# Attention plus gated FFN on one core: score banks from full-array matmuls on masked queries, spare matmuls placed by weighted streaming, other order constants, and ten split row blocks for three

## The chip, the cores and the metric

The kernel runs on one core of one Trainium2 chip. The metric is the device time of one execution in microseconds; the median of three runs before the change is 1193.59 us (1193.0 to 1194.12). The engines are TensorE (PE, with its weight loads shown apart as PEld), VectorE (DVE), ScalarE (ACT), GpSimd (POOL) and SyncE (SP), which issues the DMAs.

## The reference

```python
def _A_ref(x, wqkv, wo):                      # B=1, S=2048, D=512, H=32, Dh=16
    qkv = transpose((x @ wqkv).reshape(B, S, 3, H, Dh), 2, 0, 3, 1, 4)
    q, k, v = qkv[0], qkv[1], qkv[2]
    scores = einsum("bhqd,bhkd->bhqk", q, k) * (Dh ** -0.5)
    p = softmax(scores, axis=-1)
    o = einsum("bhqk,bhkd->bhqd", p, v)
    return transpose(o, 0, 2, 1, 3).reshape(B, S, D) @ wo

def _B_ref(x, w1, w3, w2):                    # F=1792
    h = silu(x @ w1) * (x @ w3)
    return h @ w2

xn = layernorm(x)                             # over the last axis, eps 1e-5
out = x + _A_ref(xn, wqkv, wo) + _B_ref(xn, w1, w3, w2)
```

All tensors are bfloat16. There are 32 heads of width 16, so the scores are 32 x 2048 x 2048 numbers: 2048 blocks of 128 x 512 per pass. The kernel computes them twice: once with the queries on the partitions, to find each row's maximum, and once with the keys on the partitions, for the exponentials.

## The kernel before

**Layout.** Heads go in 8 groups of four. KT and QT hold a group's four heads in four bands of 32 partitions: 16 for the head's width, then two rows (ones in KT, minus the row maximum as a high and a low part in QT), the rest without effect. A matmul on one band uses a quarter of the array's rows (a "row" matmul, 32 x 128), and up to four such can run side by side. Everything else (projections, FFN, output, and the product of probabilities and values) uses the whole array's rows (a "col" matmul); the last of these has four column bands of 17.

**Units.** The queries are cut into 4 chunks of 512 by 8 head groups; each is cut into units of 256 queries, or of 128 in the first group and the last four. This makes 73 units; units 0, 1 and 57 to 72 have 128 queries. A block of a unit is named (128-row block of queries, head).

**The two passes of a unit.** First pass (`p1_cand`, L1013): two row matmuls (L1059) write two PSUM banks of 512 scores each, and VectorE reduces both with one maximum (L1099) into `part`. Banks 0 to 3 serve this pass, two at a time. GpSimd then joins the four partial maxima (L1195 to L1215, six small operations), writes them as two rows into Z, a DMA transposes Z, and two DMAs put the rows into QT (keys QTr0 and QTr1; the marker `("AUG", u)`). The first two and the last four units take a quicker way over VectorE and TensorE (`tile_QT2`, L804). Second pass (`p2_cand`, L1281): row matmuls (L1321) write scores minus maximum, keys on the partitions, into one of banks 4 to 7; ScalarE takes the exponential into one of 34 slots of PT (L1334), or of two neighbouring banks at once when both are ready (`exp_pair`, L1364). `score_bank` (L1268) chooses the bank; MATE is how much earlier a bank next to the last queued one is treated as free (TAIL_MATE, 0.3 us, does the same after the last reduce). `tile_PV` (L1373) multiplies with the values (L572); ScalarE moves the result to U (L1428), and GpSimd normalises it with reciprocals that travel over DRAM (L1453, L1473).

**Split blocks.** For the block (1, 3) of some units (SPLIT, L344) the maximum over 2048 keys is found otherwise: two banks get the differences of two key quarters (`d_cand`, L1127: L1155 and L1158 with the negated queries QN from GpSimd), ScalarE applies Relu into RB (L1168), and a fused VectorE operation adds RB to two quarters of the scores and takes the maximum (L1088). The other head of the pair is reduced alone, two banks at a time (kind "Q"). Four reduces become two plus one fused operation.

**Tiles.** K and Q projections, V, the FFN pairs (G and U), outputs and PV are `_Tile`s of col matmuls, one of banks 4 to 7 each. `choose` (L1522) picks the next; the FFN pairs are spread over the first pass by FFN_LO and FFN_HI, and their results wait in 24 tiles of hT (NHT) for the output matmuls.

**Order.** One program writes every engine's instruction list before the launch. The loop at L1877 asks each engine's picker for its next candidate with an estimated start, and appends the earliest. Every engine runs its list strictly in order with semaphore waits. On TensorE (`pick_pe`, L1717) the candidates are: a first-pass pair a, a second-pass bank b, a split difference d, a tile's next col matmul c, and a spare matmul f (`fill_cand`, L1688: `ident` times `xnT` into a free bank; nothing reads it). Spare matmuls keep up TensorE's activity: `note_load` counts the columns that were streamed, `low_load` says whether a spare one is wanted, and `recent_cols` under RECENT_MIN lets c (which may be the spare one) go first though a row matmul is due. A_LEAD and ROW_LEAD are how early the row matmuls are due before VectorE and ScalarE need them; PACE spreads the output tiles. On GpSimd `pick_pool` (L1849) takes the first item of the queues z, ln, nx, split, nrm, ffn and pad that can start soonest.

Of the kernel before, what the change touches and what calls it, by code (L numbers as in the profile page):

```python
# [8 lines left out]
ALU = mybir.AluOpType  # L9
# [4 lines left out]
_COLD = 5.9  # L14
_VIS = {"dve": 0.138, "pool": 0.085}
# [21 lines left out]
class _Prog:  # L37
# [3 lines left out]
    def __init__(self):  # L41
        self.ops = {e: [] for e in _ENGS}
        self.reg = {}
        self.ndma = 0
        self.dma_last = [None] * _NDMA_SEMS
        self.dma_final = [0] * _NDMA_SEMS
        self.free = {e: 0.85 for e in _ENGS}
        self.rg = [0.0] * 4
        self.pe_mode = "col"
        self.pe_full = True  # L50
        self.pe_vis = 0.0
        self.act_end = 0.0
# [83 lines left out]
    def pe(self, fn, reads, writes, mode, groups, dur, name="", first=None):  # L136
# [117 lines left out]
def _build(nc, A_x, A_wqkv, A_wo, B_w1, B_w3, B_w2, out):  # L254
# [21 lines left out]
    LAZY_GAP = 0.02  # L276
# [37 lines left out]
    FFN_HI = 800  # L314
# [7 lines left out]
    LOAD_RATE = 5000.0  # L322
    LOAD_CAP = 3000.0
    LOAD_MIN = 3000.0
    RECENT = 2.9
    RECENT_MIN = 9800.0
# [3 lines left out]
    SPLIT_LO = 40  # L330
    SPLIT_END = 12
    SPLIT_STEP = 6
# [21 lines left out]
    with ctx:  # L354
# [5 lines left out]
        stats = sb("stats", [128, NT, 6], FP32)  # L360
        mv = sb("mv", [128, NT, 2], FP32)
        lnr = sb("lnr", [128, NT], FP32)
        lnb = sb("lnb", [128, NT], FP32)
        lnt = sb("lnt", [128, NT], FP32)
# [30 lines left out]
        U = sb("U", [128, NUB, 256], FP32)  # L395
        R = sb("R", [128, 2, 256], FP32)
# [58 lines left out]
        poolq = {k: [] for k in ("z", "ln", "nx", "split", "nrm", "ffn", "pad")}  # L455
# [22 lines left out]
        P.op("dve", lambda e: e.memset(wq_last[:, :, :], 0.0), writes=[("wq7",)], occ=0.3 * NPADQ)  # L478
        P.op("dve", lambda e: e.memset(bank(7), 0.0), writes=[("ps", 7)], occ=0.5)
# [533 lines left out]
        def p1_cand():  # L1013
# [42 lines left out]
            def emit():  # L1056
                def f(e):
                    for i, (j, c_) in enumerate(cells):
# [4 lines left out]
                P.pe(f, reads, writes, "row", rows, _c_mm(512) * (3 - len(rows)), name="p1_%d" % n, first="dve")  # L1063
                p1_n[0] += 1
                tokens[0] = min(tokens[0] + PACE, PACE_CAP)
                note_load(st, 1024)
# [60 lines left out]
        def d_cand():  # L1127
# [22 lines left out]
            def emit():  # L1150
# [11 lines left out]
                note_load(st, 1024)  # L1162
# [7 lines left out]
            return st, emit, rd, n  # L1170

# [109 lines left out]
        def p2_cand():  # L1281
# [17 lines left out]
            kb, j = rest[best[1]]  # L1299
            k0 = kb * kpb  # L1300
            reads = (qh_keys(qs, q0, nq, (j,)) + qt_keys(qs, q0, nq, "QTr0") + qt_keys(qs, q0, nq, "QTr1")
# [3 lines left out]
            st = P.pe_start("row", (j,), rd)  # L1305
            sl = pt_free[0]

            def emit():
                rest.pop(best[1])
# [16 lines left out]
                P.pe(f, reads, writes, "row", (j,), _c_row(nq, kpb), name="p2_%d" % n, first="act")  # L1326
                note_load(st, 512)
# [194 lines left out]
        def choose():  # L1522
# [9 lines left out]
            if outs and ok(outs[0]) and exp_unit[min(pv_u[0], NU - 1)] <= 14:  # L1532
                return outs.pop(0)
            if ffn and ok(ffn[0]):
                return ffn.pop(0)
# [52 lines left out]
        def col_cand():  # L1588
# [20 lines left out]
            def emit_part(k):  # L1609
# [11 lines left out]
                note_load(st, t.cols // 4 * k)  # L1621

            def emit():
# [5 lines left out]
                note_load(st, t.cols if t.cols < 2048 else t.cols * left // 512)  # L1629
# [22 lines left out]
        level = [0.0, 0.0]  # L1652
        recent = []

        def load_at(st):
            return level[1] - LOAD_RATE * max(0.0, st - level[0])

        def note_load(st, w):
            level[1] = min(LOAD_CAP, max(load_at(st), -LOAD_CAP) + w)
            level[0] = max(st, level[0])  # L1660
            recent.append((st, w))

        def recent_cols(st):
            while recent and recent[0][0] < st - 4.0:
                recent.pop(0)
            return sum(w for t, w in recent if t >= st - RECENT)

        def low_load(st):
            return load_at(st) < LOAD_MIN

        def warm_cand():
            for bk in (5, 4):
# [5 lines left out]
                def emit():  # L1678
# [4 lines left out]
                    note_load(st, 1024)  # L1683
# [4 lines left out]
        def fill_cand():  # L1688
# [16 lines left out]
            def emit_part(k):  # L1705
# [3 lines left out]
                note_load(st, 512 * k)  # L1709
                n_fill[0] += 1  # L1710
            return st, lambda: emit_part(4), _c_mm(512), emit_part, 4
        n_fill = [0]

# [3 lines left out]
        def pick_pe():  # L1717
# [12 lines left out]
            end = max(P.free["pe"], max(P.rg))  # L1730
            rows = []
# [12 lines left out]
            def go(x):  # L1744
                def f():
                    couple[0] = x[0]
                    x[1]()
                return x[0], f
# [9 lines left out]
            if p1_n[0] >= NP1 and b is not None:  # L1758
# [118 lines left out]
        while True:  # L1877
            assign()
            split_prep()
            best = None  # L1880
# [10 lines left out]
        P.n_fill = n_fill[0]  # L1891
        P.n_pair = n_pair[0]
# [65 lines left out]
```

## Time and profile before

| what | value |
|---|---|
| median of 3 runs | 1193.59 us |
| the profiled execution's span | 1191.2 us |
| TensorE busy | 1122.5 us (94%), mean granted clock 0.998 |
| VectorE busy | 1173.5 us (99%) |
| ScalarE busy | 1167.5 us (98%) |
| GpSimd busy | 455.5 us (38%) |
| DMA | 52.07 MB, 44 GB/s in the mean |

The span goes from the first to the last instruction of one profiled execution; the runs' times include what lies around it, and are about 2.4 us longer here. Busy time counts every moment in which at least one instruction of an engine is in flight, so an engine whose instructions overlap at their ends can look full while it could still take more. In a row of groups stand line, engine, operation, output and inputs with their shapes, the count, busy time, mean duration in ns, and the idle time before it with what ended it. In a row of windows stand the stretch and its length, then the busy time and count of PE, PEld, DVE, ACT and POOL (of those that ran, when one line is asked for), the granted clock of TensorE, and the DMA's share and rate. In a row of waits stand who waited for whom, total us, times, and the longest.

### The profile page before, as it was taken

The numbers are of one execution on the slowest core, as the hardware profiler recorded it, in microseconds if no ns is written. First come the engines' busy times: TensorE is split into PE (matmuls) and PEld (weight loads), VectorE is DVE, ScalarE is ACT, GpSimd is POOL, SyncE is SP. The second block draws the span as 40 slices with busy tenths as digits, with TensorE's granted clock in tenths as the row PEclk, the third lists the DMA queues.
The fourth block names the chain that finished last, engine by engine and source line by source line (L and its number), as shares of the span: only waits on it lengthen the run. The fifth ranks groups of instructions, "written<-read, shape, count | busy, mean of one in ns | idle before, by whom it ended". The sixth has DMA issues, their size and how long they took to land.

```text
span 1191.2 us, 33351 instructions
## 1 busy us (share of the span) xinstructions
PE 1122.5 (94%) x13807; PEld 477.7 (40%) x13964; DVE 1173.5 (99%) x1079; ACT 1167.5 (98%) x2223; POOL 455.5 (38%) x910
## 2 busy tenths in 40 slices
PE   9999999999999999999999999999899999998997
PEld 4433333333334333333333334343333333345554
DVE  8999999999999999999999999999999999999995
ACT  7899999999999999999999999999999999999998
POOL 5363743433432255344422236634222124333320
PEclk9999999999999999999999999999999999999999
DMA  6523222111111021111100122211000111000000
GB/s 185 124 62 86 66 65 80 39 33 42 36 25 38 24 70 43 36 37 29 35 20 25 36 53 49 48 42 37 23 20 15 36 28 42 24 19 20 19 18 22
DMA packets 130779, 52.07 MB, mean 44 GB/s; under 512 B 99788, under 2 KB 130628, under 8 KB 130628
## 3 DMA queue, kind: packets, MB, share of 16 engines
q1 hardware_dynamic: 130628, 49.94, 16.9%
q8 instruction: 109, 1.79, 0.6%
q14 instruction: 42, 0.34, 0.1%
HBM read 38.67 MB, written 6.74 MB: 38 GB/s over the span
## 4 chain that ended last, share of the span: by engine, by line
ACT 43%; PE 28%; DVE 22%; issue 2%; DMA 2%; POOL 1%; SPq 0%; ACTq 0%; another core or an unknown queue 0%; POOLq 0%
ACT PT L1334 29%; DVE part L1099 22%; PE ps L568 11%; PE ps L1321 8%; ACT PT L1364 7%; PE ps L1059 5%; PE ps L572 4%; ACT zg L867 1%; ACT th L861 1%; ACT U L1428 1%; DMA R<-rd 1%; ACT ub L871 1%; ACT kq L756 1%; DMA rd<-Rc 1%; ACT xnT L677 1%
## 5 line engine op out<-in xcount | busy, mean ns | idle before, releaser
L1099 DVE TENSOR_REDUCE part<-ps 128x2 f32<-128x1024 f32 x1018 | 1153.2, 1257 | 1.5 <-PE ps L1059 1.3
L1334 ACT ACTIVATE PT<-ps 128x512 bf16<-128x512 f32 x1660 | 879.2, 627 | 4.7 <-PE ps L1321 1.7
L1321 PE MATMUL ps<-QT,KT 32*128 32x256 bf16 (+1 forms) x4672 | 544.5, 259 | 10.7 <-ACT PT L1364 4.7
L1059 PE MATMUL ps<-KT,QT 32*128 32x512 bf16 x2042 | 423.9, 383 | 4.4 <-DVE part L1099 3.1
L1321 PEld LDWEIGHTS ps<-QT,KT 32*128 32x128 bf16 x4672 | 206.9, 92 | 214.9 <-issue 110.3
L1453 POOL TENSOR_TENSOR Rc<-Lc,mone 128x8 f32<-128x8 f32 (+1 forms) x69 | 105.0, 1522 | 287.2 <-DMA Lc<-U 287.1
L1364 ACT ACTIVATE PT<-ps 128x1024 bf16<-128x1024 f32 x194 | 204.4, 1078 | 0.0
L568 PE MATMUL ps<-xnT,ident 128*128 128x512 bf16 (+3 forms) x576 | 159.1, 335 | 26.1 <-DVE part L1099 6.3
L572 PE MATMUL ps<-PT,Vaug 128*17 128x256 bf16 (+1 forms) x4672 | 177.3, 261 | 4.2 <-ACT PT L1334 1.6
L1059 PEld LDWEIGHTS ps<-KT,QT 32*128 32x128 bf16 x2042 | 107.3, 91 | 122.8 <-DVE part L1099 56.7
L568 PE MATMUL ps<-xnT,w 128*128 128x512 bf16 (+3 forms) x597 | 143.8, 316 | 9.8 <-ACT U L1428 4.4
L572 PEld LDWEIGHTS ps<-PT,Vaug 128*17 128x17 bf16 x4672 | 82.2, 89 | 89.5 <-issue 68.9
L568 PEld LDWEIGHTS ps<-xnT,ident 128*128 128x128 bf16 x642 | 47.0, 97 | 99.4 <-ACT PT L1334 44.2
L568 PEld LDWEIGHTS ps<-xnT,w 128*128 128x128 bf16 x637 | 44.9, 97 | 85.7 <-issue 53.0
L568 PE MATMUL ps<-w,hT 128*128 128x512 bf16 (+3 forms) x312 | 72.1, 311 | 3.3 <-ACT U L1428 2.1
L848 POOL TENSOR_TENSOR a<-zg,ub 128x512 f32<-128x512 bf16 x56 | 64.6, 1154 | 21.8 <-ACT ub L871 21.5
L850 POOL TENSOR_TENSOR hT<-a,t 128x512 bf16<-128x512 f32 x56 | 71.0, 1268 | 2.4
L1206 POOL TENSOR_TENSOR mx<-part 128x16 f32<-128x16 f32 (+1 forms) x67 | 14.2, 211 | 140.5 <-DVE part L1099 140.2
L1473 POOL TENSOR_TENSOR wk_on<-U,R 128x256 bf16<-128x256 f32 (+1 forms) x36 | 22.9, 637 | 81.3 <-DMA R<-rd 81.2
L846 POOL TENSOR_SCALAR t<-th 128x512 f32<-128x512 bf16 x56 | 34.8, 622 | 43.8 <-ACT th L861 42.2
L1473 POOL TENSOR_TENSOR on_b<-U,R 128x256 bf16<-128x256 f32 (+1 forms) x33 | 23.4, 710 | 72.5 <-DMA R<-rd 72.4
L861 ACT ACTIVATE th<-zg 128x512 bf16<-128x512 bf16 x56 | 37.6, 671 | 0.0
(105 smaller groups left out, 552.2 us busy)
## 6 DMA issues: line engine op xcount, KB each, us to landing
w<-in_B_w_dram SPq DMA_DIRECT2D x112, 128.0 KB
R<-rd SPq DMA_DIRECT2D x55, 128.0 KB
QT<-qd SPq DMA_DIRECT2D x31, 128.0 KB
KT<-kd SPq DMA_DIRECT2D x28, 128.0 KB
PT<-in_A_x_dram SPq DMA_DIRECT2D x4, 512.0 KB
xr<-in_A_x_dram SPq DMA_DIRECT2D x16, 128.0 KB
out_dram<-osb SPq DMA_DIRECT2D x16, 128.0 KB
qd<-kq SPq DMA_DIRECT2D x15, 128.0 KB
```

Source lines behind the costliest of these rows:

```text
L568: return e.matmul(bank(bk)[:, c0 + a:c0 + b], make_lhsT(0, 128), rhs_ap(0)[:, a:b], start=start, stop=stop, **kw)
L572: ins = e.matmul(bank(bk)[32 * i:32 * i + m, c0 + a:c0 + b], make_lhsT(i), rhs if (a, b) == (0, ncols) else rhs[:, a:b], start=start, stop ...
L848: q.append(_Item(lambda e: e.tensor_tensor(a32[:, :], zg[:, ss, :], ub[:, ss, :], ALU.mult), [("zg", ss), ("ub", ss)], [("a32",)], 1.1, 1.25))
L850: q.append(_Item(lambda e: e.tensor_tensor(hT[:, hslot(idx), :], a32[:, :], t1[:, :], ALU.mult), [("a32",), ("t1",)], [("hT", hslot(idx))] ...
L861: lazyq.append(_Item(lambda e: e.activation(th[:, ss, :], zg[:, ss, :], ACTF.Tanh), [("zg", ss)], [("th", ss)], 0.52, cb=part_done))
L1059: ins = e.matmul(bank(2 * sl + i), QT[32 * j:32 * j + 32, qs, q * 128:(q + 1) * 128], KT[32 * j:32 * j + 32, g, c_ * 512:(c_ + 1) * 512], ...
L1099: redq.append(_Item(lambda e: e.tensor_reduce(dst, pair_ap.rearrange("p (a b) -> p a b", b=512), AX.X, ALU.max), writes, [("part", par, qt ...
L1321: ins = e.matmul(bank(b)[:, i * nq:(i + 1) * nq], KT[32 * j:32 * j + 32, g, (k0 + i) * 128:(k0 + i + 1) * 128], QT[32 * j:32 * j + 32, qs, ...
L1334: expq.append(_Item(lambda e: e.activation(PT[:, sl, :], bank(b), ACTF.Exp, scale=SCALE), [("ps", b)], [("PT", sl)], _c_act(512), cb=cb, e ...
L1364: return _Item(lambda e: e.activation(PT[:, s0:s1 + 1:s1 - s0, :], ps8[:, b0:b1 + 1:b1 - b0, :], ACTF.Exp, scale=SCALE), [("ps", b0), ("ps ...
L1453: poolq["nrm"].append(_Item(lambda e: e.tensor_tensor(Rc[:, pp, 0:nl], Lc[:, pp, 0:nl], mone[:, 0:nl], ALU.pow), [("Lc", pp), ("mone",)], ...
L1473: poolq["nrm"].append(_Item(lambda e: e.tensor_tensor(onorm[ob][:, g, q0:q0 + nq], U[:, us, 0:nq], R[:, pp, 0:nq], ALU.mult), [("U", us)] ...
```

## The change

The scores of a second-pass bank may also be made by a col matmul over all 128 rows: KT of all four heads against BD, a copy of the unit's QT in which the bands of the other three heads are zero. GpSimd makes four copies for each unit but the last four (`bd_prep`), two units' worth at a time, with a mask `hmask` that is written at the start. Such a wide bank (`p2_cand(True)`) is taken in place of the row bank when the recent activity is under HEAT_WIDE, or after a col matmul when ScalarE soon needs a bank and the first pass is not due.

Activity is now a weighted mean of streaming over the last 2.0 us (`heat`): 0.794 for each row band, 2.36 for banded col matmuls, 2.16 for full ones. A spare matmul is wanted while it is below HEAT_FILL = 1.5. HEAT_FORCE = 0 takes the place of RECENT_MIN, HEAT_P1 = 0 leaves the repeated first-pass matmuls unused, and HEAT_TILE = 9.0 lets FFN tiles go.

The split units go from 20 on in steps of 4 (before: from 40 in steps of 6). Some order constants change, hT has 22 tiles instead of 24, and the statistics of the layer norm lie in U.

```diff
+_HEAT_ROW, _HEAT_COL, _HEAT_FULL = 0.794, 2.36, 2.16
...
+        w = _HEAT_ROW * len(groups) if mode == "row" else _HEAT_FULL if self.pe_full else _HEAT_COL
+        self.heat.append((start, start + dur, w))
...
-    LAZY_GAP = 0.02
+    LAZY_GAP = 0.1
...
-    MATE = 0.0
+    MATE = 0.2
...
-    A_LEAD = 0.69
-    RELAX = 0.03
-    PACE = 4500
-    PACE_CAP = 6000
-    NHT = 24
+    A_LEAD = 0.76
+    RELAX = 0.0
+    PACE = 7000
+    PACE_CAP = 9000
+    NHT = 22
...
-    FFN_HI = 800
+    FFN_HI = 880
...
-    LOAD_RATE = 5000.0
-    LOAD_CAP = 3000.0
-    LOAD_MIN = 3000.0
-    RECENT = 2.9
-    RECENT_MIN = 9800.0
+    RECENT = 2.0
+    HEAT_FILL = 1.5
+    HEAT_TILE = 9.0
+    HEAT_P1 = 0
+    AGAIN = 3
+    HEAT_FORCE = 0
+    HEAT_WIDE = 1.1
...
-    SPLIT_LO = 40
+    BD_ON = 1
+    BD_END = 4
+    BD_NEAR = 0.35
+    WIDE_LEAD = 0.45
+    W_WAIT = 0.02
+    OUT_GATE = 14
+    SPLIT_LO = 20
     SPLIT_END = 12
-    SPLIT_STEP = 6
+    SPLIT_STEP = 4
...
+        BD = sb("BD", [128, 2, 4, 256], BF16)
...
+        hmask = sb("hmask", [128, 4], FP32)
...
+        P.op("dve", lambda e: e.memset(hmask[:, :], 0.0), writes=[("hmask",)], occ=0.07)
+        def head_masks(e):
+            for j in range(4):
+                ins = e.memset(hmask[32 * j:32 * j + 32, j:j + 1], 1.0)
+            return ins
+        P.op("dve", head_masks, writes=[("hmask",)], occ=0.26)
...
+        def bd_prep():
+            u = bd_next[0]
+            if u >= NU - BD_END:
+                return
+            if ("AUG", u) not in done or (u >= 2 and p2_u[0] <= u - 2):
+                return
+            bd_next[0] += 1
+            qc, g, q0, nq = units[u]
+            qs = (qc * NG + g) % 3
+            if p2_u[0] > u:
+                return
+            for j in (2, 3, 0, 1):
+                poolq["bd"].append(_Item(
+                    lambda e, j=j: e.tensor_scalar(BD[:, u % 2, j, 0:nq], QT[:, qs, q0:q0 + nq], hmask[:, j:j + 1], 0.0,
+                                                   ALU.mult, ALU.add),
+                    [("hmask",)] + qh_keys(qs, q0, nq) + qt_keys(qs, q0, nq, "QTr0") + qt_keys(qs, q0, nq, "QTr1"),
+                    [("BD", u % 2, j)], 0.12 + nq / 1000.0, cb=lambda op, j=j: done.add(("BD", u, j))))
...
-        def p2_cand():
+        def p2_cand(wide=False):
...
+            whole = ()
+            if BD_ON and u < NU - BD_END:
+                whole = [k for k, (kb, j) in enumerate(rest[:4]) if ("BD", u, j) in done]
+            if wide and not whole:
+                return None
...
+            st = P.pe_start("col", None, rd) if wide else P.pe_start("row", (j,), rd)
...
+                if wide:
+                    parts = [col_groups(b, lambda i, z=32, a=a: KT[:, g, (k0 + a) * 128 + 32 * i:(k0 + a) * 128 + 32 * i + z],
+                                        lambda i: BD[:, u % 2, j, 0:nq], nq, c0=a * nq,
+                                        own=P.pe_mode == "col" and not P.pe_full) for a in range(kpb)]
...
+        def heat(st):
+            h = P.heat
+            while h and h[0][1] < st - 6.0:
+                h.pop(0)
+            return sum(w * (min(b_, st) - max(a_, st - RECENT)) for a_, b_, w in h
+                       if b_ > st - RECENT and a_ < st) / RECENT
         def low_load(st):
-            return load_at(st) < LOAD_MIN
+            return heat(st) < HEAT_FILL
...
+            if b is not None and red_n[0] < NP1 and heat(max(end, b[2])) < HEAT_WIDE:
+                w = p2_cand(True)
+                if w is not None:
+                    b = w
+                    warm = True
...
+            if b is not None and P.pe_mode == "col" and not warm:
+                w = p2_cand(True)
+                if w is not None:
+                    near = max(P.free["dve"] + sum(it.occ for it in redq) - A_LEAD, a[2]) if a is not None else 1e9
+                    if near > max(w[0], end) + BD_NEAR:
+                        if w[0] <= end + W_WAIT and P.free["act"] + 0.476 * len(expq) - WIDE_LEAD <= w[0]:
+                            return w[0], w[1]
+                        if x is b and not fits(c, late + TOL):
+                            return w[0], w[1]
             k = fits(c, late + TOL)
-            if not k and recent_cols(c[0]) < RECENT_MIN and c[0] <= end + URG_WAIT:
+            if not k and heat(c[0]) < HEAT_FORCE and c[0] <= end + URG_WAIT:
                 k = min(2, c[4]) if len(c) > 3 else 9
...
-            for k in ("z", "ln", "nx", "split", "nrm", "ffn", "pad"):
+            for k in ("z", "ln", "nx", "split", "bd", "nrm", "ffn", "pad"):
```

More of the change, by code (lines that the diff above doesn't have):

```diff
@@ L454, in _build @@
         dveq = []
[L455 removed]
+        poolq = {k: [] for k in ("z", "ln", "nx", "split", "bd", "nrm", "ffn", "pad")}
         spq = []
@@ L1056, in emit @@
             def emit():
+                again = 1
+                if n >= N_HEAD and kind == "R":
+                    slack = P.free["dve"] + sum(it.occ for it in redq) - st - 0.25
+                    while again < AGAIN and heat(st) + 0.35 * (again - 1) / RECENT < HEAT_P1 and slack > (again + 1) * _c_mm(512):
+                        again += 1
                 def f(e):
-                    for i, (j, c_) in enumerate(cells):
+                    for i, (j, c_) in list(enumerate(cells)) * again:
                         ins = e.matmul(bank(2 * sl + i), QT[32 * j:32 * j + 32, qs, q * 128:(q + 1) * 128],
@@ L1325, in f, with fw @@
                     return ins
-                P.pe(f, reads, writes, "row", (j,), _c_row(nq, kpb), name="p2_%d" % n, first="act")
-                note_load(st, 512)
+                if wide:
+                    parts = [col_groups(b, lambda i, z=32, a=a: KT[:, g, (k0 + a) * 128 + 32 * i:(k0 + a) * 128 + 32 * i + z],
+                                        lambda i: BD[:, u % 2, j, 0:nq], nq, c0=a * nq,
+                                        own=P.pe_mode == "col" and not P.pe_full) for a in range(kpb)]
+                    def fw(e):
+                        for p_ in parts:
+                            ins = p_(e)
+                        return ins
+                    fw.full = parts[0].full
+                    P.pe(fw, reads, writes, "col", None, kpb * _c_mm(nq), name="w2_%d" % n, first="act")
+                    n_wide[0] += 1
+                else:
+                    P.pe(f, reads, writes, "row", (j,), _c_row(nq, kpb), name="p2_%d" % n, first="act")
                 def cb(op):
@@ L1744, in go @@
             def go(x):
+                if warm and x is b:
+                    return x[0], x[1]
                 def f():
```

52 lines of the change are left out of this document (22 added, 30 removed).

## The prediction

> **What bounds the kernel now.** I read the page first, then the groups, the windows of the long middle stretch, and the timeline of VectorE and ScalarE at its edges.
>
> ```profile
> span 1191.2 us, 33351 instructions
> PE 1122.5 (94%) x13807; PEld 477.7 (40%) x13964; DVE 1173.5 (99%) x1079; ACT 1167.5 (98%) x2223; POOL 455.5 (38%) x910
> ACT 43%; PE 28%; DVE 22%; issue 2%; DMA 2%; POOL 1%; SPq 0%; ACTq 0%; another core or an unknown queue 0%; POOLq 0%
> L1099 DVE TENSOR_REDUCE part<-ps 128x2 f32<-128x1024 f32 x1018 | 1153.2, 1257 | 1.5 <-PE ps L1059 1.3
> L568 PE MATMUL ps<-xnT,ident 128*128 128x512 bf16 (+3 forms) x576 | 159.1, 335 | 26.1 <-DVE part L1099 6.3
> ```
>
> Three engines look full, and the chain of waits hops between them, so no single one explains the end. VectorE's claim is the hard one: 1018 row maxima, before which it sat idle 1.5 us in all. The timeline gives the price of one by start-to-start distances (columns: start, duration, engine, line, operation):
>
> ```profile
> 13.21 27.31 DVE L1099 TENSOR_REDUCE part<-ps 128x2 f32<-128x1024 f32 x24 [1.04 <-PE ps L1059]
> ...
> 719.10 4.64 DVE L1099 TENSOR_REDUCE part<-ps 128x2 f32<-128x1024 f32 x4
> 723.62 1.25 DVE L1088 CUSTOM_DVE_ANT_0 RB<-ps,RB 128x1024 f32<-128x1024 f32 x1
> 724.76 0.12 DVE L1088 DVE_READ_ACCUMULATOR2_ANT part<- 128x1 f32 x1
> 724.76 5.78 DVE L1099 TENSOR_REDUCE part<-ps 128x2 f32<-128x1024 f32 x5
> ...
> 1162.17 8.00 DVE L1099 TENSOR_REDUCE part<-ps 128x2 f32<-128x1024 f32 x7
> 1170.21 0.17 DVE L1235 TENSOR_REDUCE negm<-part 128x4 f32<-128x16 f32 x1
> ```
>
> From 719.10 to 723.62 four reduces start: 1.13 us each. The whole phase, 13.21 to 1170.21, holds 1018 reduces and three fused ones (L1088): 1157.0/1021 = 1.133 us each. A fused one takes 724.76 - 723.62 = 1.14 us. VectorE cannot go faster here except by doing fewer.
>
> ScalarE's 98% is softer: its instructions overlap by about 0.15 us, which hides small gaps. The distances between starts show what one really occupies:
>
> ```profile
> 823.20 0.67 ACT L1168 ACTIVATE RB<-ps 128x512 f32<-128x512 f32 x1
> 823.68 0.68 ACT L1334 ACTIVATE PT<-ps 128x512 bf16<-128x512 f32 x1
> 824.16 0.70 ACT L1168 ACTIVATE RB<-ps 128x512 f32<-128x512 f32 x1
> 824.63 1.14 ACT L1364 ACTIVATE PT<-ps 128x1024 bf16<-128x1024 f32 x1
> 825.54 1.21 ACT L1334 ACTIVATE PT<-ps 128x512 bf16<-128x512 f32 x2
> ...
> 901.83 0.42 ACT L1428 ACTIVATE U<-ps 128x256 f32<-128x256 f32 x1
> 902.10 0.64 ACT L1334 ACTIVATE PT<-ps 128x512 bf16<-128x512 f32 x1
> ```
>
> A single bank costs 0.477 us (823.20 to 824.63 is three), a pair 0.91, a 256-wide evacuation 0.27. The windows of the stretch 100 to 1170.2 us count them: all of ScalarE's instructions, then L1334 (single), L1364 (pair), L1428 (evacuation of U); the last two rows are L1334 and L1364 after VectorE's last reduce.
>
> ```profile
> 100.00:1170.20 1070.20, 1014.42 (x12488) 426.14 (x12628) 1070.00 (x952) 1064.94 (x2025) 408.03 (x813) 1.00 0.15 37
> 100.00:1170.20 1070.20, 835.79 (x1582) 1.00 0.15 37
> 100.00:1170.20 1070.20, 182.84 (x174) 1.00 0.15 37
> 100.00:1170.20 1070.20, 25.60 (x66) 1.00 0.15 37
> 1170.20:1191.20 21.00, 5.48 (x8) 0.88 0.08 27
> 1170.20:1191.20 21.00, 12.97 (x13) 0.88 0.08 27
> ```
>
> 174 x 0.91 + 66 x 0.27 + 1785 x 0.477 = 1028 us of work in 1070: some 42 us (4%) are gaps. ScalarE is thus close behind VectorE. When the last reduce ends it still has 8 + 2 x 13 = 34 banks of exponentials to do, and these set the tail:
>
> ```profile
> 1171.77 0.29 DVE L817 TENSOR_SCALAR QT<-ps 128x128 bf16<-128x128 f32 x1 [0.38 <-PE ps L568]
> ...
> 1184.96 0.87 ACT L1334 ACTIVATE PT<-ps 128x512 bf16<-128x512 f32 x1
> ```
>
> The last exponential ends at 1185.8, the span at 1191.2. The last unit alone has 16 banks, so 18 of the 34 are backlog. The kernel is VectorE-bound until 1170 and ScalarE-bound after.
>
> **The change part by part.**
>
> *Split blocks.* The new range gives eleven units, 20 to 60 by 4; unit 60 has only one row block and no block (1, 3), so ten are real, where there were three (four listed, the last void in the same way). Each replaces four reduces by two and a fused one: 2 x 1.133 - 1.14 = 1.13 us less. Seven more: **-7.9 us of VectorE**. In return each asks two Relu banks of ScalarE (L1168): 7 x 2 x 0.477 = **+6.7 us of ScalarE**; and four row matmuls more, less the two it saves.
>
> *Pairing.* The preference for a neighbouring bank goes from 0 to 0.2 us. In the stretch 174 pairs hold 348 of 1582 + 348 banks, 18%; in the tail, where the preference is already 0.3, they hold 26 of 34, 76%. A pair saves 2 x 0.477 - 0.91 = 0.04 us. Bounds: no more pairs, 0 us; the tail's share, 1930 x 0.58/2 = 560 more pairs, -22 us. The new value is nearer to the tail's, but mates are scarcer while a tile and the reduces also hold banks; I take a third of the banks, 150 more pairs, **-6 us of ScalarE**. Relus and pairs cancel.
>
> *Wide scores.* A bank's scores may be made by a full-array matmul on queries in which the other three heads are zero. No score changes. What it occupies: (columns as above)
>
> ```profile
> 820.56 0.60 PE L568 MATMUL ps<-xnT,ident 128*128 128x512 bf16 x2
> 821.10 0.39 PE L1321 MATMUL ps<-QT,KT 32*128 32x256 bf16 x4
> 821.43 0.34 PE L568 MATMUL ps<-xnT,ident 128*128 128x384 bf16 x1
> ```
>
> Two 512-column full matmuls take 0.60 us and their last alone 0.38, so one streams 0.22 us. Four 256-column row matmuls (two banks, in two row groups at once) take 0.39 from first start to last end, as long as one 512-column matmul alone. So a wide bank costs 0.22 us of the array, a row bank between 0.11 and 0.22. At worst, with every bank wide, that is 2048 x 0.11 = 225 us more of TensorE; at best it is a gain, since a wide bank between two full-array groups saves the change of form. Its cover are the spare matmuls: 576 pieces, 159 us by the group's row, overlapping tails included; the 512s alone, 341 by the grouping by shape, make 341 x 0.22 = 75 us of streaming. A wide bank does useful work where a spare one did none. I take nothing for it on TensorE.
>
> ```profile
> L568 PE MATMUL ps<-xnT,ident 128*128 128x512 bf16 x341 | 117.9, 385 | 19.7 <-ACT PT L1334 4.9 <-DVE part L1099 4.1 <-ACT PT L1364 3.2
> L1122 POOL TENSOR_SCALAR QN<-QT 128x128 bf16<-128x128 bf16 x3 | 0.9, 304 | 0.2
> L544 POOL TENSOR_SCALAR wq_last<-wq 128x256 bf16<-128x256 bf16 x1 | 0.4, 407 | 0.0
> POOL Rc L1453 <- DMA Lc<-U: 287.1, 49, 11.6
> PEld ps L1321 <- ACT PT L1334: 50.7, 166, 0.4
> ```
>
> The masked queries are made on GpSimd: 69 units x 4, 55 of them 256 wide at 0.407 us, 14 of them 128 wide at 0.304: 220 x 0.407 + 56 x 0.304 = 107 us, from 455 to 562 of 1191. That fits into its idle time. But the copy waits for the unit's row maxima to land by DMA, and behind it on GpSimd stand the maxima chain of the next unit, the normalisations and the FFN products; GpSimd already stands 287 us behind one such landing. Cost between 0 and (if one copy in four is late by its own 0.4 us and the units' chain passes it on) 69 x 0.4 = 28 us; I take 0, since a unit is prepared a whole unit ahead.
>
> The Trainium skill, "TensorE: Matmul & The Clock Gate", in the table "Why this matters for your kernels", says that a K=32 matmul takes as long alone as a K=128 one and gains only by running beside others: it speaks against wide banks. The row at 821.10 agrees. Its price is the 225 us bound above; it would bind only if few spare matmuls went.
>
> *Spare matmuls and order.* The old rule could force a spare or tile group ahead of a row bank that was already due; the new limit of 0 never forces. That is where ScalarE's gaps should shrink: TensorE's weight loads for scores waited 166 times for a bank (50.7 us), so a free bank is often the last thing to arrive, and what TensorE runs then decides the gap. Bounds: gaps unchanged, 42 us; none, 0. VectorE's phase is 7.9 us shorter, with ScalarE's work unchanged, so ScalarE keeps its place only if gaps fall to 34 us. I take that: it is the nearer end. The other constants (lead, pacing, FFN end 800 to 880, 22 hidden tiles for 24) issue no instructions; their cover is VectorE's queue of reduces. The mask's few memsets stand before VectorE's first statistics:
>
> ```profile
> 4.82 1.29 DVE L605 BATCH_NORM_STATS2 stats<-PT 128x6 f32<-128x512 bf16 x2 [2.51 <-DMA PT<-in_A_x_dram]
> ```
>
> 2.51 us of waiting for the input cover them.
>
> *Sum.* 1191.2 - 7.9 + 0 (tail as now: 34 banks left) = 1183.3 us of span. The median, 1193.6, is 2.4 us above the span, so **1185.7**; a little of the shift being lost, I say **1186.5 us**.
>
> **The rivals.**
>
> *ScalarE becomes the bound; slower.* Place: the backlog of exponentials. If neither pairs nor gaps improve, the 6.7 us of Relu appear at the end of ScalarE's chain, whatever VectorE saves: 1193.6 + 6.7 = 1200.3. It decides from the point where pairs and closed gaps together give less than 6.7 us. For it: the tail is ScalarE's already. Against: 42 us of gaps. Closing about 6.7 of them without more gives no change.
>
> *The backlog shrinks as well.* With many pairs, ScalarE arrives at the last reduce with only the last unit to do: 18 banks less, but never under its 16. Query rows ready at 1171.77 + 0.29, 1.9 us after the last reduce; 16 banks as 8 pairs, 7.3; from the last exponential to the end, 5.4; some 0.5 between: 15 us of tail for 21: 1193.6 - 7.9 - 6 = 1179.7. That is the floor.
>
> *The clock falls.*
>
> ```profile
> 840.00:860.00 20.00, 17.83 (x219) 6.75 (x216) 20.00 (x19) 20.00 (x36) 5.68 (x12) 1.00 0.10 25
> 1185.00:1192.00 7.00, 0.44 (x16) 0.32 (x17) 1.79 (x5) 0.83 (x2) 0.00 (x0) 0.58 0.06 19
> ```
>
> The granted clock is 1.00 wherever TensorE is busy and 0.58 where it does almost nothing. Fewer spare matmuls could bring it down inside the run. Without 159 us of spares TensorE is busy (1122 - 159)/1191 = 81%; at 0.58 each us carries 0.58/0.81 = 0.72 of its work and loses 0.28. A tenth of the run at that clock costs 33 us: about 1220. Against: no window of the run shows a fall under load.
> The skill's page named above, Part 1, has the clock halve only after a whole window of about 3.4 us idle; by that rule nothing falls here and the forecast stands.
>
> *Masked copies come late.* GpSimd late, TensorE waiting in order, VectorE starved: up to +28 us, about 1205 at half of that.
>
> **How the numbers follow.** Forecast 0.47 (own range 1183 to 1190); backlog shrinks 0.15; no change, gaps just paying for the Relus, 0.08; ScalarE-bound 0.18; clock 0.07; late copies 0.05. A measurement of this kernel tells about 0.2%, 2.4 us, from no change. Faster 0.62, same 0.08, slower 0.30. The range runs from the floor, 1180, to 1203: it takes in the ScalarE case and leaves out the clock and the worst of the copies.
>
> **What would show it.** Right: 1004 reduces and 10 fused ones at 1.13 us, the last ending near 1162, idle before them still a few us; 20 Relu banks; more than 250 pairs; about 34 banks left; granted clock 1.00. Wrong: more than 40 banks left after the last reduce (ScalarE), idle before L1099's reduces of over 5 us (TensorE or GpSimd late), a clock below 0.98 inside the run.

## The result and the profile after

The change makes the kernel slower: 1196.53 us in the median of 20 runs (1195.04 to 1200.62) against 1193.58 us (20 runs, 1193.0 to 1195.44), a ratio of 1.0026 (95% interval 1.0019 to 1.0032). The profiled execution's span is 1195.4 us, 4.2 us longer than before; with 1197.31 us it is one of the longer runs.

These are lines of the page of the kernel after: the span, the engines, the chain, and the groups that answer to those shown of before (L1123 was L1099, L1398 was L1334, L1428 was L1364).

```profile
span 1195.4 us, 34945 instructions
PE 1116.0 (93%) x14395; PEld 524.9 (44%) x14537; DVE 1167.7 (98%) x1086; ACT 1169.1 (98%) x2221; POOL 575.6 (48%) x1200
ACT 52%; PE 23%; DVE 22%; issue 2%; POOL 1%; ACTq 0%; another core or an unknown queue 0%; POOLq 0%
L1123 DVE TENSOR_REDUCE part<-ps 128x2 f32<-128x1024 f32 x1004 | 1138.5, 1204 | 3.0 <-PE ps L1084 1.5
L1398 ACT ACTIVATE PT<-ps 128x512 bf16<-128x512 f32 x1632 | 876.5, 689 | 5.0 <-PE ps L1373 2.2
L1428 ACT ACTIVATE PT<-ps 128x1024 bf16<-128x1024 f32 x208 | 227.4, 1121 | 0.0
L1210 POOL TENSOR_SCALAR BD<-QT,hmask 128x256 bf16<-128x256 bf16 (+1 forms) x276 | 122.0, 457 | 181.0 <-DMA QT<-Zs 149.1
L587 PE MATMUL ps<-xnT,ident 128*128 128x512 bf16 (+3 forms) x292 | 84.4, 335 | 18.4 <-ACT PT L1428 8.7
```

VectorE did what was forecast: 1004 reduces for 1018. But ScalarE's share of the chain went from 43% to 52%, and pairs rose only from 194 to 208. For comparison, the single exponentials and the pairs on the page of the kernel before:

```profile
L1334 ACT ACTIVATE PT<-ps 128x512 bf16<-128x512 f32 x1660 | 879.2, 627 | 4.7 <-PE ps L1321 1.7
L1364 ACT ACTIVATE PT<-ps 128x1024 bf16<-128x1024 f32 x194 | 204.4, 1078 | 0.0
```

On the timeline of the kernel after, the first row below is VectorE's last reduces; the second starts when that phase is over.

```profile
1156.70 8.00 DVE L1123 TENSOR_REDUCE part<-ps 128x2 f32<-128x1024 f32 x7
1164.73 0.17 DVE L1278 TENSOR_REDUCE negm<-part 128x4 f32<-128x16 f32 x1
```

The last reduce ends 5.5 us earlier than before (1164.7 for 1170.2), of the 7.9 us that the splits save. Now the windows of the same kernel, from 100 us to that point and from there to the end. The first row has all engines; the next two pairs of rows are the single exponentials (L1398) and the pairs (L1428), each before and after the last reduce; the last is the evacuation of U (L1492).

```profile
100.00:1164.70 1064.70, 998.88 (x12894) 466.00 (x13017) 1063.25 (x952) 1057.52 (x2007) 520.19 (x1082) 1.00 0.15 37
100.00:1164.70 1064.70, 823.32 (x1540) 1.00 0.15 37
1164.73:1195.40 30.67, 16.79 (x28) 0.99 0.08 24
100.00:1164.70 1064.70, 200.31 (x185) 1.00 0.15 37
1164.73:1195.40 30.67, 14.48 (x13) 0.99 0.08 24
100.00:1164.70 1064.70, 28.87 (x65) 1.00 0.15 37
```

Behind the last reduce 28 + 2 x 13 = 54 banks of exponentials are left or under way, where there were 34 by the same count (by starts alone it is 52, the number that some expectations below use). Twenty more banks at 0.46 to 0.49 us are over 9 us; VectorE was 5.5 us earlier. The same engine's timeline near the end shows what a bank really costs it:

```profile
1182.21 0.93 ACT L1398 ACTIVATE PT<-ps 128x512 bf16<-128x512 f32 x1
1182.69 1.37 ACT L1428 ACTIVATE PT<-ps 128x1024 bf16<-128x1024 f32 x1
1183.59 0.96 ACT L1398 ACTIVATE PT<-ps 128x512 bf16<-128x512 f32 x1
1184.07 1.40 ACT L1428 ACTIVATE PT<-ps 128x1024 bf16<-128x1024 f32 x1
1184.97 0.98 ACT L1398 ACTIVATE PT<-ps 128x512 bf16<-128x512 f32 x1
...
1187.74 2.51 ACT L1398 ACTIVATE PT<-ps 128x512 bf16<-128x512 f32 x4
```

Add start and duration to get the ends: 1183.14, 1184.06, 1184.55, 1185.47, 1185.95. A single bank ends 0.49 us after the one before it, a pair 0.92, though the starts are 0.48 and 0.90 apart. Starts run ahead, and the durations grow by about 13 ns with each instruction for as long as ScalarE is never short of work; behind a gap they are back near 0.6 us. That the mean single went from 627 to 689 ns is the same thing seen from afar: a fuller engine, not a slower one (in both kernels the ends of singles are 0.49 us apart).

By ends, ScalarE's work in the stretch before was 1785 x 0.49 + 174 x 0.92 + 66 x 0.27 = 1053 us of 1070, not 1028: 17 us of gaps, where the prediction saw 42. After the change it is 1757 x 0.49 + 185 x 0.92 + 65 x 0.27 = 1049 of 1065: 16 us. The prices are rounded, so the 17 is good to a few us; between kernels the count compares better. The gaps did not close.

### The profile page after: what moved, and what is told of

It reads as the page before. It is cut to its first block, busy times and chain, and to the rows that moved or that the text cites. A ratio compares the mean times of both kernels' runs of the same rounds, so it can differ in the third digit from the quotient of the medians.

```text
span 1195.4 us, 34945 instructions
## 1 busy us (share of the span) xinstructions
PE 1116.0 (93%) x14395; PEld 524.9 (44%) x14537; DVE 1167.7 (98%) x1086; ACT 1169.1 (98%) x2221; POOL 575.6 (48%) x1200
## 4 chain that ended last, share of the span: by engine, by line
ACT 52%; PE 23%; DVE 22%; issue 2%; POOL 1%; ACTq 0%; another core or an unknown queue 0%; POOLq 0%
ACT PT L1398 35%; DVE part L1123 21%; ACT PT L1428 10%; PE ps L587 9%; PE ps L591 6%; PE ps L1084 4%; PE ps L1373 4%; ACT zg L886 1%; ACT ub L890 1%; ACT th L880 1%; ACT U L1492 1%; PE ps L1734 1%; ACT RB L1191 1%; ACT kq L775 0%; ACT xnT L696 0%
## 5 line engine op out<-in xcount | busy, mean ns | idle before, releaser
L1123 DVE TENSOR_REDUCE part<-ps 128x2 f32<-128x1024 f32 x1004 | 1138.5, 1204 | 3.0 <-PE ps L1084 1.5
L1398 ACT ACTIVATE PT<-ps 128x512 bf16<-128x512 f32 x1632 | 876.5, 689 | 5.0 <-PE ps L1373 2.2
L1373 PE MATMUL ps<-QT,KT 32*128 32x256 bf16 (+1 forms) x3582 | 464.2, 258 | 10.9 <-ACT PT L1428 3.2
L1373 PEld LDWEIGHTS ps<-QT,KT 32*128 32x128 bf16 x3582 | 168.9, 92 | 181.6 <-issue 68.2
L1428 ACT ACTIVATE PT<-ps 128x1024 bf16<-128x1024 f32 x208 | 227.4, 1121 | 0.0
L1210 POOL TENSOR_SCALAR BD<-QT,hmask 128x256 bf16<-128x256 bf16 (+1 forms) x276 | 122.0, 457 | 181.0 <-DMA QT<-Zs 149.1
L587 PE MATMUL ps<-BD,KT 128*128 128x256 bf16 (+1 forms) x738 | 123.9, 263 | 5.1 <-ACT PT L1428 3.0
L587 PE MATMUL ps<-xnT,ident 128*128 128x512 bf16 (+3 forms) x292 | 84.4, 335 | 18.4 <-ACT PT L1428 8.7
L587 PE MATMUL ps<-w,hT 128*128 128x128 bf16 (+3 forms) x345 | 78.8, 297 | 3.8 <-ACT U L1492 3.0
L587 PEld LDWEIGHTS ps<-BD,KT 128*128 128x128 bf16 x738 | 58.6, 98 | 34.6 <-ACT PT L1428 7.2
L591 PE MATMUL ps<-BD,KT 128*32 128x256 bf16 (+1 forms) x1408 | 61.0, 261 | 0.0
L587 PEld LDWEIGHTS ps<-xnT,ident 128*128 128x128 bf16 x332 | 27.2, 97 | 67.5 <-ACT PT L1428 20.6
```

What stands on the lines that cost most here:

```text
L587: return e.matmul(bank(bk)[:, c0 + a:c0 + b], make_lhsT(0, 128), rhs_ap(0)[:, a:b], start=start, stop=stop, **kw)
L591: ins = e.matmul(bank(bk)[32 * i:32 * i + m, c0 + a:c0 + b], make_lhsT(i), rhs if (a, b) == (0, ncols) else rhs[:, a:b], start=start, stop ...
L1123: redq.append(_Item(lambda e: e.tensor_reduce(dst, pair_ap.rearrange("p (a b) -> p a b", b=512), AX.X, ALU.max), writes, [("part", par, qt ...
L1210: lambda e, j=j: e.tensor_scalar(BD[:, u % 2, j, 0:nq], QT[:, qs, q0:q0 + nq], hmask[:, j:j + 1], 0.0, ALU.mult, ALU.add),
L1373: ins = e.matmul(bank(b)[:, i * nq:(i + 1) * nq], KT[32 * j:32 * j + 32, g, (k0 + i) * 128:(k0 + i + 1) * 128], QT[32 * j:32 * j + 32, qs, ...
L1398: expq.append(_Item(lambda e: e.activation(PT[:, sl, :], bank(b), ACTF.Exp, scale=SCALE), [("ps", b)], [("PT", sl)], _c_act(512), cb=cb, e ...
```

## The experiments

Each ratio is against the kernel before on the same chip, with its 95% interval. Edits are to the kernel after unless said otherwise.

**Three split blocks in the new order (e1)**

```diff
-    SPLIT_LO = 20
+    SPLIT_LO = 40
-    SPLIT_STEP = 4
+    SPLIT_STEP = 6
```

> The kernel after with the three split blocks of before. Theory S (ScalarE was already full, its banks end 0.49 us apart, and each split block asks two more of it): 14 Relu banks fewer are 6.9 us less of ScalarE and 7.9 us more of VectorE; last reduce near 1172.5, fewer than 40 banks left behind it, time 1189 to 1193. Rival O (the new order and the wide banks cost the time, splits are indifferent): 1195 to 1198, as the kernel after.

Seven runs gave two values: 1192.73 and 1192.93, and five from 1198.03 to 1199.73 (median of all seven 1198.15, ratio 1.0040, 1.0027 to 1.0054). The profiled execution, with a span of 1191.2, belongs to the low one: 29 banks left, last exponential over at 1185.1. There theory S holds. The high value it does not explain; but the granted clock was 1.00 in the two low runs and 0.992 to 0.994 in the five high ones, and e6 and e10 take that up.

**Ten split blocks in the old order (e2; edit to the kernel before)**

```diff
-    SPLIT_LO = 40
+    SPLIT_LO = 20
-    SPLIT_STEP = 6
+    SPLIT_STEP = 4
```

> The kernel before with ten split blocks and nothing else. Theory S: ScalarE gets 6.9 us more and had no room: 1198 to 1202, last reduce near 1162, more than 50 banks left behind it. Rival O: VectorE's 7.9 us are gained: 1185 to 1189.

1202.17 us, ratio 1.0072 (1.0059 to 1.0084): slower by 8.8 us with nothing changed but the splits. The reduces ended at 1165.8. The groups of ScalarE:

```profile
L1334 ACT ACTIVATE PT<-ps 128x512 bf16<-128x512 f32 x1714 | 903.2, 640 | 6.6 <-PE ps L1321 3.3 <-PE ps L1059 0.2
L1364 ACT ACTIVATE PT<-ps 128x1024 bf16<-128x1024 f32 x167 | 178.8, 1111 | 0.0
```

Fourteen more Relus at 0.49 are 6.9 us. Pairs fell from 194 to 167, each lost one costing 2 x 0.49 - 0.92 = 0.06 us: 1.6 more. Together 8.5 of the 8.8. The 7.9 us that VectorE was spared do not show in the time at all, though its last reduce ended 4.4 us earlier than before.

**The load alone (e12; edit to the kernel before)**

```diff
+                if idx % 4 == 0:
+                    lazyq.insert(len(lazyq) - 1, _Item(lambda e: e.activation(th[:, ss, :], zg[:, ss, :], ACTF.Tanh),
+                                                       [("zg", ss)], [("th", ss)], 0.52))
```

> The kernel before, with its three split blocks, and 14 of its 56 tanh activations done twice (the same values into the same tile): 14 x 0.52 = 7.3 us more of ScalarE, nothing else added, nothing taken from VectorE. The row of the forecast (42 us of ScalarE's time between 100 and 1170 us are gaps) would let it in for nothing: at most 1 us. If the gaps are what the distances between ends say (a bank every 0.49 us, some 20 us of gaps that the waits for banks keep open), the time grows by 5 to 10 us, 1198 to 1203, as it did with seven more split blocks.

1205.33 us, ratio 1.0098 (1.0081 to 1.0115): 12.1 us for 7.3 us of work, above even the upper guess. Pairs fell to 172, which is 1.3; the other 3.5 us fit the gaps, which the changed order widened (1071.3 - (1824 x 0.49 + 150 x 0.92 + 65 x 0.27) = 22 us, for 17). The claim that ScalarE had 42 us to spare falls here. The windows of this kernel behind its last reduce (1171.3), singles and pairs:

```profile
1171.33:1203.40 32.07, 13.61 (x26) 0.91 0.08 23
1171.33:1203.40 32.07, 15.29 (x15) 0.91 0.08 23
```

56 banks left, with VectorE's phase ending only 1 us later than before. Next to e2 it also prices VectorE's 7.9 us, only roughly, since the two orders differ: 1205.3 - 1202.2 = 3 us.

**The Relus cut short (e5, e9)**

```diff
-                expq.append(_Item(lambda e: e.activation(RB[:, h, :], bank(b), ACTF.Relu),
-                                  [("ps", b)], [("RB", h)], _c_act(512), cb=cb, exp=(b, h, None)))
+                expq.append(_Item(lambda e: e.activation(RB[:, h, 0:32], bank(b)[:, 0:32], ACTF.Relu),
+                                  [("ps", b)], [("RB", h)], _c_act(32), cb=cb, exp=(b, h, None)))
```

In e5 the cost told to the ordering program stays `_c_act(512)`, so the order is unchanged; in e9 it is `_c_act(32)`. The paired form is cut in the same way, and RB is cleared once at the start; the other columns of the differences are left out. In an unbroken run a cut Relu ends 0.09 us behind the instruction before it, 0.4 us less than a full one.

> The kernel after in its own order, with each Relu of the split blocks cut to the first 32 of 512 columns (the rest of the differences is left out; RB is cleared once at the start). Only ScalarE's 20 Relus get shorter, by about 0.4 us each, 8 us together. Theory S (ScalarE is full, and its end is the kernel's end): 1187 to 1191. Rival G (ScalarE's gaps absorb the Relus, the time comes from elsewhere): 1195 to 1198.

> As the run with the Relus cut to 32 columns, but the program that writes the order now also counts them as short, so that it puts more score banks ahead of the last reduce. (The rest of the differences is again left out.) In the run before this one the order was the old one, and 52 banks stayed behind the last reduce although ScalarE had less to do. Theory L (ScalarE's load counts through the written order: it decides how many banks lie behind the last reduce): at most 42 banks left, time 1187 to 1192. Rival X (what the Relus occupy does not matter at all): 50 banks or more, 1195 to 1198.

e5 gave 1196.56 us, ratio 1.0028 (1.0017 to 1.0040): nothing gained, against theory S as I had put it, and the number of rival G. Its windows behind the last reduce (1163.9), singles and pairs:

```profile
1163.90:1194.60 30.70, 16.32 (x28) 0.97 0.08 24
1163.90:1194.60 30.70, 14.14 (x13) 0.97 0.08 24
```

The same 54 banks are left as in the kernel after. TensorE runs its list in order, and how many score banks stand in it behind the last first-pass pair is written before the launch; a ScalarE that is done sooner only waits. The gaps show it: 1063.9 - (1738 x 0.49 + 185 x 0.92 + 65 x 0.27 + 20 x 0.09) = 23 us before the last reduce, for 16, so nearly 7 of the 8 us saved became gaps. With the cost told (e9) the kernel took 1192.84 us, ratio 0.9999 (0.9991 to 1.0008), some 3 us less than the kernel after, each against its own runs of before:

```profile
1161.90:1190.20 28.30, 13.15 (x21) 0.94 0.08 23
1161.90:1190.20 28.30, 16.14 (x14) 0.94 0.08 23
```

49 banks are left, more than the 42 that theory L allowed, and the median lies just above the 1187 to 1192 it named. Yet it is the plainest run of the study. Its 20 cut Relus are some 1.8 us and its 16 pairs fewer than before cost 1.0, against 2.9 us for the six Relus of the kernel before: **equal work on ScalarE, 7.9 us less on VectorE, and the same time**.

**Old order constants (e8)**

```diff
-    LAZY_GAP = 0.1
+    LAZY_GAP = 0.02
-    MATE = 0.2
+    MATE = 0.0
-    A_LEAD = 0.76
-    RELAX = 0.0
-    PACE = 7000
-    PACE_CAP = 9000
+    A_LEAD = 0.69
+    RELAX = 0.03
+    PACE = 4500
+    PACE_CAP = 6000
-    FFN_HI = 880
+    FFN_HI = 800
```

> The kernel after with MATE, LAZY_GAP, A_LEAD, RELAX, PACE, PACE_CAP and FFN_HI as in the kernel before. Theory S: these constants put no work on ScalarE and MATE makes few pairs, so pairs stay within 30 of 208 and the time within 1194 to 1198. Rival M (the preference for neighbours makes the pairs): at least 50 pairs fewer, 3 us more.

1194.90 us (1193.86 to 1198.02), ratio 1.0016 (1.0008 to 1.0025), and again 208 pairs:

```profile
L1428 ACT ACTIVATE PT<-ps 128x1024 bf16<-128x1024 f32 x208 | 223.5, 1107 | 1.0 <-PE ps L1373 1.0
```

With the preference for a neighbouring bank at 0, and six other constants back, no pair is lost. My reading, not tested by itself: a pair needs two banks waiting at once, and ScalarE gets its banks one by one.

**Without wide banks, and without spare matmuls (e3, e4)**

```diff
-    BD_ON = 1
+    BD_ON = 0          (e3)
-    HEAT_FILL = 1.5
-    HEAT_WIDE = 1.1
+    HEAT_FILL = 0.0    (e4)
+    HEAT_WIDE = 0.0    (e4)
```

> The kernel after with no wide bank taken; the masked copies are still made. Theory S says nothing of it by itself; if wide banks only replace spare matmuls the time stays within 2 us of 1196.5. Theory W (wide banks keep ScalarE fed when TensorE is in full-array form): ScalarE's gaps grow and the time is above 1201. Rival O (wide banks take the array from others): below 1193.

> The kernel after with no spare matmuls once the run is under way and no wide bank forced for activity (wide banks after a full-array matmul remain). Theory S: ScalarE's work is the same, so 1193 to 1197 unless gaps close; clock stays 1.00. Rival C (the clock needs the streaming): mean granted clock below 0.95 and time above 1215.

e3 took 1214.59 to 1222.77 us in four runs, ratio 1.0205 (1.018 to 1.023), and 1233.47 in a fifth, the profiled one; e4 took 1272.17 us, ratio 1.0664 (1.0647 to 1.0681). In e4 the clock is the cause: 0.865 in its profiled execution, with VectorE and ScalarE idle where it falls. In e3 it is most of it: the clock was 0.979 to 0.987 in the four runs and 0.965 in the fifth, and a straight line through the five times reaches about 1204 us at the 0.998 of the kernel after. The 8 us that are left would then not be the clock's. Theory W, a ScalarE less well fed, named a time above 1201 and may be right for them; no run here separates the two. Four neighbouring windows of e4:

```profile
200.00:234.30 34.30, 32.31 (x404) 13.58 (x402) 34.30 (x31) 34.08 (x64) 18.49 (x37) 1.00 0.24 62
234.30:244.60 10.30, 10.23 (x120) 3.79 (x118) 8.15 (x8) 7.82 (x14) 4.03 (x9) 0.50 0.08 21
244.60:248.00 3.40, 2.62 (x24) 0.82 (x22) 3.40 (x4) 3.40 (x7) 2.34 (x3) 0.99 0.36 78
248.00:251.40 3.40, 3.40 (x16) 0.85 (x16) 2.75 (x3) 2.40 (x5) 0.00 (x0) 0.50 0.09 24
```

The clock goes to exactly half, in stretches of 3.4 us or multiples of it, and VectorE and ScalarE then stand idle for about a fifth of the time or more (they are busy 8.15 and 7.82 of 10.3 us). It falls although TensorE is busy 32.31 of the 34.3 us before, with no idle stretch in them above 0.7 us. So the spare matmuls serve the clock, and e3 shows that the wide banks do too: with none taken, the same rule for spares no longer holds it, though it then puts in 409 full-array pieces for 332 (by their weight loads, as some matmul records are missing).

The Trainium skill, "TensorE: Matmul & The Clock Gate", Part 1, has the same halving and the same window of about 3.4 us, but its table lets the clock fall after an idle window; here it falls under a TensorE that the profile shows busy, and the measurement decides.

**Where the two values come from (e6, e10)**

```diff
     SPLIT_LO = 40, SPLIT_STEP = 6          (both, as e1)
-    HEAT_FILL = 1.5
+    HEAT_FILL = 1.7                        (e6)
-            return heat(st) < HEAT_FILL
+    HEAT_TAIL = 3.0                    (e10)
+            return heat(st) < (HEAT_FILL if p1_n[0] < NP1 else HEAT_TAIL)      (e10)
```

> The kernel after with three split blocks, and spare matmuls wanted below an activity of 1.7 instead of 1.5. The same kernel at 1.5 gave 1192.8 in two runs and 1198 to 1200 in five. Theory F (in those five the clock fell for some windows of 3.4 us, because the recent activity lies close to what holds the clock): all runs between 1191 and 1195, none near 1198. Rival N (the two values have another cause, splits or order): two values again, or all near 1198.

> The kernel after with three split blocks, and spare matmuls wanted below an activity of 3.0 once the last first-pass pair is issued (before that 1.5, same order). It puts in only a few more of them. Theory T (the second value near 1198 of the run with three split blocks is the clock falling behind the last reduce, and TensorE's load there decides): all runs 1191 to 1195. Rival P (whether the clock falls there depends on where its window begins in that execution, and a few spares more do not help): again two values, near 1193 and near 1198.

e6 gave 1196.92 us in one cluster (1195.87 to 1197.79), ratio 1.0029 (1.0018 to 1.0039): not the 1191 to 1195 of theory F: it has only 170 pairs for the 222 of e1, worth 3 us at 0.06, and the clock was 0.994 to 0.997 in all eight runs; in the profiled execution it fell behind the last reduce all the same. e10 gave two values again: five runs from 1192.92 to 1193.55, one at 1195.73, and six from 1198.26 to 1200.43 (median of all twelve 1197.0, ratio 1.0028, 1.0013 to 1.0043). The granted clock was 1.00 in the five, 0.997 in the one and 0.993 or 0.994 in the six. Its profiled execution caught a fall; windows of e10:

```profile
1160.00:1172.50 12.50, 12.10 (x280) 7.69 (x282) 11.23 (x18) 12.50 (x28) 1.49 (x4) 1.00 0.04 9
1172.50:1186.10 13.60, 12.79 (x136) 5.32 (x132) 1.28 (x5) 9.98 (x19) 0.40 (x1) 0.50 0.00 1
```

and the same windows of e1, whose profiled execution had none:

```profile
1160.00:1172.50 12.50, 12.40 (x281) 7.71 (x275) 11.42 (x17) 12.50 (x28) 1.43 (x3) 1.00 0.04 9
1172.50:1186.10 13.60, 13.60 (x296) 7.20 (x294) 3.85 (x12) 12.57 (x24) 0.46 (x1) 1.00 0.04 12
```

Up to 1172.5 us the two run alike. Then e10 has half the clock for 13.6 us, issues 136 matmuls for 296, and ends 5.3 us later. The order up to there is the same. The two values are thus the clock's; why it falls in one execution of a kernel and not in another is not shown. That a window of fixed length begins elsewhere in each execution would do it, but that is argued only. The kernel after meets falls too. In its profiled execution one window went to half, and VectorE stands idle for some of it (windows of the kernel after):

```profile
795.00:798.70 3.70, 3.28 (x29) 1.33 (x27) 3.70 (x4) 3.70 (x7) 2.29 (x5) 1.00 0.08 18
798.70:802.10 3.40, 3.40 (x38) 0.92 (x36) 2.99 (x3) 2.54 (x5) 2.96 (x6) 0.50 0.02 6
802.10:810.00 7.90, 7.19 (x113) 3.21 (x112) 7.55 (x7) 7.75 (x15) 3.43 (x10) 1.00 0.06 11
```

ScalarE is short by 0.86 us in it and 0.15 just behind it, some 1 us in all. One such window accounts for a part of the 4.2 us of span; the best of the 20 runs, 1195.04, is still 2 us over the best of before, and the nine runs with a clock of 0.999 have a median of 1196.2.

**A middle course (e7, e11)**

```diff
     SPLIT_LO = 24, SPLIT_STEP = 6, TOL = 0.02, HEAT_WIDE = 0.9, W_WAIT = 0.12, A_LEAD = 0.80   (both)
+    HEAT_FILL = 1.7                                                                        (e7)
+    HEAT_FILL = 1.6, behind the last pair 2.2, WIDE_LEAD = 0.35, MATE = 0.1, TAIL_MATE = 0.2   (e11)
```

> The kernel after with six real split blocks (units 24 to 54 in steps of 6), spare matmuls below 1.7, and four order constants changed (TOL 0.02, HEAT_WIDE 0.9, W_WAIT 0.12, A_LEAD 0.80). Theory S and F together: ScalarE and VectorE are nearer to balance and the clock holds: 1188 to 1193. If order does not matter and only the split count does, halfway between three and ten: 1193 to 1196.

> The looser six-split kernel (1191.4 before) with spare matmuls below 1.6 instead of 1.7, 2.2 behind the last first-pass pair, WIDE_LEAD 0.35, MATE 0.1 and TAIL_MATE 0.2. Theory L: fewer spares leave ScalarE fewer gaps, about 32 banks behind the last reduce, 1188 to 1191. If the clock falls more often with fewer spares: 1192 to 1196 with a wider spread.

e7, with six real split blocks, is the one kernel that beats both: 1191.41 us (1189.96 to 1194.08), ratio 0.9988 (0.9979 to 0.9997), with 11 + 2 x 12 = 35 banks left behind its last reduce; the margin is small, and which of its settings gives it is not separated. e11 reached 1189.65 in its best run, but lost it to the clock in others (median 1193.34, up to 1197.13; ratio 0.9997, 0.9987 to 1.0007; clock 0.998 in the best run, 0.989 in the longest); in its profiled execution two stretches inside the run were at half clock.

## Why the prediction was wrong

The forecast was 1186.5 us with own range 1183 to 1190; the time fell inside the wide range, on the other side of no change. The prediction's own sign of being wrong came, more than 40 banks left (54), and its "more than 250 pairs" did not (208).

- *VectorE's share was right.* 1004 reduces and 10 fused ones, as counted. The last one ended at 1164.7 for a forecast "near 1162"; 3.0 us of idle time before the reduces, for 1.5, are a part of what is missing.
- *The step that failed is ScalarE's gaps*: "174 x 0.91 + 66 x 0.27 + 1785 x 0.477 = 1028 us of work in 1070: some 42 us (4%) are gaps", and from it "ScalarE keeps its place only if gaps fall to 34 us. I take that". The 0.477 is the distance of starts in a short run; by ends it is 0.49, which over 2000 instructions is 25 us. There were 17 us, and there still are 16 after. e12 shows that nothing fits into them: 7.3 us more of ScalarE cost 12.1. The prediction looked for the closing of gaps where weight loads wait for a bank; but in that row TensorE waits until ScalarE frees one, which tells of a full ScalarE, and these waits grew, from 50.7 us in 166 to 65.7 in 239.
- *Pairs were mis-sized*: 150 more were taken, 14 came, worth 0.8 us instead of 6 (at the 0.06 us that ends give). The share in the tail, which I took for the effect of the preference, rather comes from banks queuing there; e8 has the same 208 without the preference.
- *The sum by the rival "ScalarE becomes the bound"*, which had 0.18: Relus 14 x 0.49 = +6.9, pairs -0.8; the last exponential moved from 1185.8 to 1190.25, +4.4, so about 1.7 us were taken from gaps. It had said 1200.3, with no gap used; the mechanism is this one. In the old order, e2, it comes within 2 us of that number.
- *"VectorE-bound until 1170 and ScalarE-bound after" was the wrong picture.* VectorE had next to no gaps, and ScalarE none that could be filled, and e9 with equal ScalarE work ended with the kernel before although VectorE was done earlier. What ScalarE cannot do beside the reduces stands behind them.
- *Wide banks at nothing* was right only in its sum. They did replace spares (292 full-array pieces on record and 84.4 us for 576 and 159.1; by weight loads 332 for 642), and most of their worth is the clock, as e3 shows: without them the time rose by 2%.
- *The clock rival* was put down as unlikely, at 0.07, and for the change as it stands it costs no more than about 1 us in the profiled execution. Its price was somewhat high: 33 us for a tenth of the run at 0.58 is 7.9 us for each per cent of clock, and e4 lost 13.5% of the clock and 79 us, 5.8 for each. The 0.58 was the mean of a window; where the clock falls it goes to 0.50. But "no window of the run shows a fall under load" was no safety: the kernel after is nearer to the edge, as its fall at 798.7 shows.
- *Late masked copies* did not show: GpSimd waited 149.1 us for the query rows in front of the copies, and no wait of TensorE for them is in the list. Each copy took 0.457 us in the mean, for 0.407 and 0.304 taken.

## What to carry to other kernels

Where two engines are both near full, price a trade between them on the one that finishes last, and measure its cost per instruction by the ends of a long unbroken run of them, not by starts. An order that is written out ahead fixes where the work lies: shortening an instruction gains nothing until the order is made again with its new cost. Matmuls that only keep the clock up can be replaced by useful ones that fill the array, but look at several executions before the margin is called enough.

## What the runs showed of the hardware

The clock of TensorE falls to half in windows of 3.4 us though TensorE is at work: in the rows in front of the falls above it is busy 32.31 of 34.3 us and 2.62 of 3.4 (e4), and 12.10 of 12.5 (e10). Without spare matmuls the mean clock was 0.865 and the time 6.6% longer, without wide banks 0.979 to 0.987 and 2.1%. Both kernels lack full-array matmuls that the kernel after has; that this decides, and not the small idle stretches, was not tested by itself. Executions of one program can differ in it by 5 us and more (e10: near 1193 us at a clock of 1.00, 1198 to 1200 at 0.993). And ScalarE's durations in the profile grow, from 0.6 to above 1.0 us for one 128 x 512 bank, by about 13 ns with each, for as long as it is fed without a break, while the ends stay 0.49 us apart.
